# GpSimd's two passes over each converted weight piece are made as two half-width operations each

## The chip, the cores and the metric

The kernel runs on one core of a Trainium2 chip. The metric is the device time of one execution in microseconds; the median of three runs of the kernel before is 585.58 us.

## The reference

Three stages follow each other on 3072 tokens of 256 features. All is computed in float32 precision; the weights of the last two stages arrive as float64 numbers.

```python
# 1. decayed linear attention, chunk by chunk (batch 4, 8 heads, 768 positions, head 32, state 16)
M = (C @ B.T) * exp(cum_i - cum_j) * causal
y = M @ x + (C @ state) * exp(cum)
state = exp(sum(log a)) * state + sum_j decay_j * outer(B_j, x_j)
# 2. a layer of three products and a maximum (256 -> 768 -> 256)
h = maximum(maximum(y @ w1, y @ w2), y @ w3);  z = h @ w_out
# 3. a layer with a rational function (256 -> 2048 -> 256)
h = z @ w_in
g = (a0 + a1*h + a2*h**2 + a3*h**3) / (1 + |b0|*|h| + |b1|*h**2 + 1e-6)
out = g @ w_out2
```

## The kernel before

The sequence is cut into six groups `g` of 128 positions in four batches, so a group is 512 tokens. Stage 1 (attention) runs first, for all groups, in units `u` of four heads: TensorE makes scores (`s`) and decay differences (`d`), ScalarE the exponential `e`, VectorE the product `m` (L503), TensorE the output `y` from `m`. The matmuls of stages 2 and 3 then run group by group: stage 2 in blocks of 128 features (`pg`, or `ph` for group 0, the maximum into `xa` on VectorE at L726, its high and low part `hhi`, `hlo`), stage 3 in 16 blocks `k` of 128 features (`ph`, the rational function, its parts `ghi`, `glo`, the output `po`). A product of two float32 numbers is made of three matmuls of high and low parts (L644 to L646).

The weights come in 28 pieces of 256 by 256 float64 numbers: nine of `w1` to `w3`, three of the first output matrix (`wo1`), eight of `win`, eight of the second output matrix (`wo2`). Each is loaded as 32-bit halves (`wraw`, three buffers) and turned into a float32 number `a` (tile `wa`, two buffers) and its parts `hi` and `lo`, in `plan_conv`. On 128 partitions and 512 columns a piece takes: ScalarE, absolute value of the upper half (L246); VectorE, clamp (L247); ScalarE, scaled lower half into `we` (L249); VectorE, shift and mask (L250) and sign (L253); GpSimd, integer add (L256); ScalarE, the high part (L257, recorded at the helper's L196); GpSimd, the low part (L258). In the text below these are the steps of a piece: the VectorE steps L247, L250 and L253, the add L256 and the low part L258. A piece's add needs its L253, its high part needs the whole add, its low part needs the high part. The `wa` buffer of a piece is free for the piece after next only when its low part is done.

The order on every engine is fixed when the program is built. `Plan.op` records each operation with an engine and a cost, reads and writes of tiles; `Plan.emit` then walks through time with these costs and picks on each engine, among the operations that are ready, the one that is due first. Two operations that write the same tile are kept in order. The attention's operations all stand ahead of those of stages 2 and 3; the pieces (phase None) may stand anywhere, and so they lie between the attention's operations and between those of the first group in stages 2 and 3. Each engine runs its list in order, so an operation whose input is late holds everything behind it.

Of the kernel before, what the change touches and what calls it, by code (L numbers as in the profile page):

```python
# [9 lines left out]
F32 = mybir.dt.float32  # L10
# [4 lines left out]
ALU = mybir.AluOpType  # L15
# [141 lines left out]
def decay_attention_max_moe_rational_moe(  # L157
# [19 lines left out]
    act, dve, pool, pe = nc.scalar, nc.vector, nc.gpsimd, nc.tensor  # L177
# [16 lines left out]
    def copy(e, o, i):  # L194
        if e is act:
            act.activation(out=o, in_=i, func=AF.Copy)  # L196
        else:
            e.tensor_copy(out=o, in_=i)
# [14 lines left out]
    def plan_conv(plan, tok, nm, src, k0, c0):  # L213

        if nm == "wo2":
            hi, lo = (lambda i=i: wsb[nm, k0 // 2][i] for i in range(2))
        else:
            hi, lo = (lambda i=i: wsb[nm][i][:, k0:k0 + 2, c0:c0 + 256] for i in range(2))
        shape = [128, 2, 256]
        wide = src.dtype != F32  # L220
        raw = plan.tile("wraw", 3, lambda: cvr.tile(shape + [2], U32, tag="wraw", name="wraw") if wide
                        else cvr.tile(shape, F32, tag="wraw", name="wst"))
        rows = slice(128 * k0, 128 * k0 + 256)
        if not wide:
            plan.op("dma", 0.73, lambda: nc.sync.dma_start(
                out=raw.t, in_=src[rows, c0:c0 + 256].rearrange("(k p) n -> p k n", p=128)), [], [raw])
            plan.op("act", 0.52, lambda: copy(act, hi(), raw.t), [raw], [tok])
            plan.op("pool", 1.23, lambda: pool.tensor_tensor(out=lo(), in0=raw.t, in1=hi().bitcast(F32),
                                                             op=ALU.subtract), [raw], [tok])
            return  # L230
        a = plan.tile("wa", 2, lambda: cva.tile(shape, U32, tag="wa", name="wa"))
        e = plan.tile("we", 2, lambda: cve.tile(shape, U32, tag="we", name="we"))
        af = lambda: a.t.bitcast(F32)
        low, high = (lambda: raw.t[:, :, :, 0]), (lambda: raw.t[:, :, :, 1])
        raws[0] += 1
        first = f"w{raws[0]}" in FIRST

        plan.op("dma", 1.46, lambda: nc.sync.dma_start(
            out=raw.t.rearrange("p k n t -> p k (n t)"),
            in_=src.bitcast(U32)[rows, 2 * c0:2 * c0 + 512].rearrange("(k p) n -> p k n", p=128)), [], [raw],
            FIRST.index(f"w{raws[0]}") - 1000.0 if first else 6.0 + PIECE * raws[0],
            behind=[cum_t] if raws[0] < 4 and not first else ())
        plan.op("act", 0.67, lambda: act.activation(out=af(), in_=high().bitcast(F32), func=AF.Abs), [raw], [a])  # L246
        plan.op("dve", 0.41, lambda: dve.tensor_scalar(  # L247
            out=af(), in0=af(), scalar1=F64_LOW, scalar2=F64_HIGH, op0=ALU.max, op1=ALU.min), [], [a])
        plan.op("act", 0.67, lambda: act.activation(out=e.t, in_=low(), func=AF.Copy, scale=2.0 ** -29), [raw], [e])  # L249
        plan.op("dve", 0.41, lambda: dve.tensor_scalar(  # L250
            out=a.t, in0=a.t, scalar1=3, scalar2=0x3FFFFFF8,
            op0=ALU.logical_shift_left, op1=ALU.bitwise_and), [], [a])
        plan.op("dve", 0.68, lambda: dve.scalar_tensor_tensor(  # L253
            out=a.t, in0=high(), scalar=0xC0000000, in1=a.t,
            op0=ALU.bitwise_and, op1=ALU.bitwise_or), [raw], [a])
        plan.op("pool", 1.3, lambda: pool.tensor_tensor(out=a.t, in0=a.t, in1=e.t, op=ALU.add), [e], [a])  # L256
        plan.op("act", 0.6, lambda: copy(act, hi(), af()), [a], [tok])  # L257
        plan.op("pool", 1.3, lambda: pool.tensor_tensor(out=lo(), in0=af(), in1=hi().bitcast(F32),  # L258
                                                        op=ALU.subtract), [a], [tok])

    for nm in ("w1", "w2", "w3"):
        w_alloc(nm, KD, DF1)
# [3 lines left out]
    plan = Plan()  # L266
    op = plan.op
# [36 lines left out]
    def w_piece(nm, src, k0, c0):  # L304
        wt[nm, k0, c0] = mark()
        plan_conv(plan, wt[nm, k0, c0], nm, src, k0, c0)
# [53 lines left out]
    for i in range(2):  # L360
        for f in range(2):
            e = "dve" if f else "pool"
# [41 lines left out]
    for p in range(3):  # L404
        src = pcv if p == 0 else (lambda p=p: cr(p - 1))
        op("act", 0.3, lambda p=p, src=src: copy(act, cs[:, p], src()), [pc if p == 0 else cr_t], [cs_t])
        if p < 2:
            op("dve", 0.34, lambda p=p, src=src: dve.tensor_tensor(out=cr(p), in0=src(), in1=cs[:, p],
                                                                   op=ALU.subtract),
# [8 lines left out]
    def load_cum(g):  # L418
# [12 lines left out]
        out=sel.rearrange("r (q n f) -> r q n f", q=2, f=4),  # L431
# [160 lines left out]
    for s in range(NS_ALL + LEAD + 3):  # L592
# [5 lines left out]
        if 0 <= u < NS_ALL:  # L598
            g, k = divmod(u, NU)
# [8 lines left out]
        if 0 <= u < NS_ALL:  # L608
            g, k = divmod(u, NU)
# [63 lines left out]
    for s in range(NG * F2 + OL):  # L673
        g, k = divmod(s, F2)
# [287 lines left out]
```

## Time and profile before

| what | value |
|---|---|
| median of three runs (lowest, highest) | 585.58 us (583.31, 587.23) |
| profiled execution: time, span | 585.64 us, 583.9 us |
| busy share: PE, PEld, DVE, ACT, POOL | 96%, 71%, 90%, 75%, 73% |
| chain that ended last | PE 52%, DVE 21%, POOL 14%, issue 5%, DMA 4% |

PE is TensorE, PEld its weight loads, DVE is VectorE, ACT ScalarE, POOL GpSimd, SP the engine that issues the transfers. Busy shares are means over stages with different limits: the steps of the pieces lie between 10 and 157 us, and from there on the three other engines work beside a TensorE that has no gap up to 525 us. The span is 1.74 us shorter than the execution's time. Rows name the line of the kernel, the engine, the operation, and the output and input tiles.

### The profile page before, as it was taken

Reading aid. Unit: us, or ns where it says so; the run is one execution under the profiler, and the core shown is the slowest. Engines: PE = TensorE matmul, PEld = TensorE weight load, DVE = VectorE, ACT = ScalarE, POOL = GpSimd, SP = SyncE. Lnnn points to the kernel's source line nnn. Section 1 sums busy time; section 2 is a strip of 40 time slices with the busy share of each in tenths; the row PEclk is TensorE's granted clock in tenths of the full one; section 3 lists DMA queues with packets and bytes.
Section 4 is the critical chain, followed back from the end, with each engine's and each line's share of the span. In section 5 each row is a group of like instructions: output and inputs, shape, how many; then the busy total and the mean of one; then the engine's idle time right before and its main releaser. Section 6 shows DMA issues by size and latency. Waiting matters only on the chain.

```text
span 583.9 us, 8072 instructions
## 1 busy us (share of the span) xinstructions
PE 562.1 (96%) x2758; PEld 412.9 (71%) x2758; DVE 525.6 (90%) x775; ACT 436.8 (75%) x756; POOL 424.5 (73%) x354
## 2 busy tenths in 40 slices
PE   8988998899899999999999999999999999999997
PEld 3334343677688888888888888888888888886663
DVE  6999999699799989989889889989898889988996
ACT  5675777565678787878777877788787776788883
POOL 2565576488778867696667777687767997869983
PEclk9998999999999999999999999999999999999999
DMA  7885774533000000100000001000000010000000
GB/s 235 241 276 189 242 241 140 179 112 108 0 1 0 27 12 0 37 0 20 19 1 36 1 0 38 1 1 36 1 0 2 1 37 0 1 0 33 5 0 36
DMA packets 19043, 33.70 MB, mean 58 GB/s; under 512 B 3523, under 2 KB 4027, under 8 KB 19003
## 3 DMA queue, kind: packets, MB, share of 16 engines
q1 hardware_dynamic: 19003, 33.20, 17.7%
q8 instruction: 21, 0.34, 0.3%
q14 instruction: 19, 0.16, 0.1%
HBM read 27.27 MB, written 5.91 MB: 57 GB/s over the span
## 4 chain that ended last, share of the span: by engine, by line
PE 52%; DVE 21%; POOL 14%; issue 5%; DMA 4%; ACT 2%; SPq 1%; POOLq 0%; DVEq 0%; ACTq 0%
PE pg L644 7%; PE pg L645 7%; PE pg L646 7%; PE ph L644 5%; PE ph L645 5%; PE ph L646 5%; PE po L645 5%; PE po L646 5%; PE po L644 4%; DVE wa L253 2%; POOL glo L847 2%; DVE wa L247 2%; DVE wa L250 2%; DVE m L503 2%; POOL v L813 2%
## 5 line engine op out<-in xcount | busy, mean ns | idle before, releaser
L847 POOL TENSOR_TENSOR glo<-w,ghi 128x512 fp32r<-128x512 f32 x80 | 105.5, 1319 | 26.7 <-ACT ghi L196 26.7
L644 PE MATMUL pg<-xhi,w_hi 128*128 128x512 f32 x202 | 79.1, 392 | 2.2 <-DVE xa L726 1.6
L645 PE MATMUL pg<-xlo,w_hi 128*128 128x512 f32 x202 | 78.7, 390 | 0.0
L646 PE MATMUL pg<-xhi,w_lo 128*128 128x512 f32 x202 | 78.6, 389 | 0.0
L196 ACT ACTIVATE ghi<-w 128x512 fp32r<-128x512 f32 x80 | 50.5, 632 | 26.5 <-PE po L646 18.3
L834 ACT ACTIVATE pr<-v,qc 128x512 f32<-128x512 f32 x83 | 57.3, 691 | 17.5 <-POOL v L813 11.1
L256 POOL TENSOR_TENSOR wa<-wa,we 128x512 uint32<-128x512 uint32 x28 | 36.9, 1316 | 43.2 <-DVE wa L253 43.2
L291 POOL TENSOR_TENSOR hlo<-xa,hhi 128x512 fp32r<-128x512 f32 x36 | 50.3, 1398 | 20.2 <-ACT hhi L196 20.1
L644 PE MATMUL ph<-yhi,win_hi 128*128 128x512 f32 x160 | 62.5, 391 | 1.5 <-DVE w L832 1.5
L645 PE MATMUL ph<-ylo,win_hi 128*128 128x512 f32 x160 | 62.4, 390 | 0.8 <-DVE ylo L291 0.8
L645 PE MATMUL po<-glo,wo_hi 128*128 128x512 f32 x160 | 62.4, 390 | 0.4 <-POOL glo L847 0.4
L644 PE MATMUL po<-ghi,wo_hi 128*128 128x512 f32 x160 | 62.3, 389 | 0.0
L646 PE MATMUL ph<-yhi,win_lo 128*128 128x512 f32 x160 | 62.2, 389 | 0.0
L646 PE MATMUL po<-ghi,wo_lo 128*128 128x512 f32 x160 | 62.2, 389 | 0.0
L839 DVE SCALAR_TENSOR_TENSOR pr<-w,co,pr 128x512 f32<-128x512 f32 x83 | 62.0, 747 | 0.0
L813 POOL TENSOR_TENSOR v<-t,v 128x512 f32<-128x512 f32 x44 | 57.9, 1317 | 2.8
L836 DVE SCALAR_TENSOR_TENSOR v<-v,pr 128x512 f32<-128x512 f32 x83 | 56.3, 679 | 3.4 <-ACT pr L835 3.4
L841 DVE SCALAR_TENSOR_TENSOR w<-v,pr 128x512 f32<-128x512 f32 x83 | 56.4, 679 | 0.7
L835 ACT ACTIVATE pr<-pr 128x512 f32<-128x512 f32 x86 | 50.5, 588 | 1.0
L726 DVE TENSOR_TENSOR xa<-xa,pg 128x512 f32<-128x512 f32 x67 | 45.5, 679 | 3.8 <-ACT xa L196 2.7
L644 PEld LDWEIGHTS pg<-xhi,w_hi 128*128 128x128 f32 x202 | 37.9, 188 | 11.8 <-DVE xa L726 2.4
L646 PEld LDWEIGHTS pg<-xhi,w_lo 128*128 128x128 f32 x202 | 37.9, 188 | 7.9
(166 smaller groups left out, 1484.4 us busy)
## 6 DMA issues: line engine op xcount, KB each, us to landing
wraw<-in_wo_dram SPq DMA_DIRECT2D x11, 512.0 KB
wraw<-in_w_dram SPq DMA_DIRECT2D x9, 512.0 KB
wraw<-in_win_dram SPq DMA_DIRECT2D x8, 512.0 KB
xn<-in_xn_dram SPq DMA_DIRECT2D x6, 512.0 KB
out_dram<-ob SPq DMA_DIRECT2D x12, 256.0 KB
xt_d<-xo SPq DMA_DIRECT2D x10, 256.0 KB
xst<-xt_d SPq DMA_DIRECT2D x10, 256.0 KB
bt<-in_bz_dram SPq DMA_DIRECT2D x6, 256.0 KB
```

Source lines behind the costliest of these rows:

```text
L196: act.activation(out=o, in_=i, func=AF.Copy)
L291: lambda: e.tensor_tensor(out=lo.t, in0=src(), in1=hi.t.bitcast(F32), op=ALU.subtract),
L644: pe.matmul(dst, wh, hi, start=first, stop=False)
L645: pe.matmul(dst, wh, lo, start=False, stop=False)
L646: pe.matmul(dst, wl, hi, start=False, stop=last)
L813: pop(1.23, lambda: pool.tensor_tensor(out=f(v), in0=f(t1), in1=f(v), op=ALU.mult), [t1], [v])
L834: aop(0.62, lambda: act.activation(out=f(r), in_=f(v), func=AF.Ln, bias=qc), [v], [r])
L835: aop(0.48, lambda: act.activation(out=f(r), in_=f(r), func=AF.Exp, scale=-1.0), [], [r])
L836: dop(0.61, lambda: dve.scalar_tensor_tensor(out=f(v), in0=f(v), scalar=QC, in1=f(r), op0=ALU.add, op1=ALU.mult), [r], [v])
L839: dop(0.61, lambda: dve.scalar_tensor_tensor(out=f(r), in0=f(w), scalar=c(0), in1=f(r), op0=ALU.add, op1=ALU.mult), [w], [r])
L841: dop(0.61, lambda: dve.scalar_tensor_tensor(out=f(w), in0=f(v), scalar=2.0, in1=f(r), op0=ALU.subtract, op1=ALU.mult), [v, r], [w])
L847: pop(1.23, lambda: pool.tensor_tensor(out=f(lo), in0=f(w), in1=f(hi).bitcast(F32), op=ALU.subtract), [w, hi], [lo])
```

## The change

The add and the low part of a piece, one GpSimd operation of 512 columns each, are made as two of 256 columns each. The loop index `k` picks the half along the tile's middle axis. The recorded cost is 0.7 for each half where it was 1.3 for the whole. The halves of one step write the same tile, so the plan keeps them in order, but it may put other operations between them. The high part still waits for both halves of the add.

```diff
-        plan.op("pool", 1.3, lambda: pool.tensor_tensor(out=a.t, in0=a.t, in1=e.t, op=ALU.add), [e], [a])
+
+        for k in range(2):
+            plan.op("pool", 0.7, lambda k=k: pool.tensor_tensor(
+                out=a.t[:, k], in0=a.t[:, k], in1=e.t[:, k], op=ALU.add), [e], [a])
         plan.op("act", 0.6, lambda: copy(act, hi(), af()), [a], [tok])
-        plan.op("pool", 1.3, lambda: pool.tensor_tensor(out=lo(), in0=af(), in1=hi().bitcast(F32),
-                                                        op=ALU.subtract), [a], [tok])
+        for k in range(2):
+            plan.op("pool", 0.7, lambda k=k: pool.tensor_tensor(
+                out=lo()[:, k], in0=af()[:, k], in1=hi()[:, k].bitcast(F32), op=ALU.subtract), [a], [tok])
```

Lines behind the change stand four lower in the changed kernel (L503 becomes L507, L726 becomes L730); its add is L258 and its low part L262.

The plan's walk is taken with other costs and more operations, so the orders change on all engines up to the first blocks of stage 3. On GpSimd, early in the attention, the order before takes the pieces one after the other, add (L256) and low part (L258); `ct` is an operation of the attention:

```order
L256 TENSOR_TENSOR wa_205<-wa_205,we_210 128x512
L258 TENSOR_TENSOR w1_lo_87<-wa_205,w1_hi_86 128x2x256
L256 TENSOR_TENSOR wa_255<-wa_255,we_270 128x512
L258 TENSOR_TENSOR w2_lo_89<-wa_255,w2_hi_88 128x2x256
L256 TENSOR_TENSOR wa_310<-wa_310,we_283 128x512
L453 TENSOR_TENSOR ct_324<-ct_324,e0_368 128x512
```

At the same place the changed order is this (add L258, low part L262):

```order
L258 TENSOR_TENSOR wa_205<-wa_205,we_210 128x256 x2
L262 TENSOR_TENSOR w1_lo_87<-wa_205,w1_hi_86 128x256 x2
L258 TENSOR_TENSOR wa_255<-wa_255,we_271 128x256 x2
L262 TENSOR_TENSOR w2_lo_89<-wa_255,w2_hi_88 128x256
L258 TENSOR_TENSOR wa_312<-wa_312,we_284 128x256
L262 TENSOR_TENSOR w2_lo_89<-wa_255,w2_hi_88 128x256
```

The second half of the second piece's low part now stands behind the first half of the third piece's add. In the same way, a second half of a low part stands behind a half of the next piece's add at nine of the 28 pieces, six of them in the attention.

On VectorE, at the end of the attention (last `m`) and the begin of stage 2 (`xa`), the order before is:

```order
L253 SCALAR_TENSOR_TENSOR wa_1299<-wraw_1184,wa_1299 128x512
L247 TENSOR_SCALAR wa_1310<-wa_1310 128x512
L503 TENSOR_TENSOR m_1333<-s_1301,e_1322 128x512
L250 TENSOR_SCALAR wa_1310<-wa_1310 128x512
L503 TENSOR_TENSOR m_1340<-s_1302,e_1325 128x512
L253 SCALAR_TENSOR_TENSOR wa_1310<-wraw_1215,wa_1310 128x512
L726 TENSOR_TENSOR xa_1431<-xa_1431,pg_1419 128x512
```

There the changed order has, up to its first `xa`:

```order
L507 TENSOR_TENSOR m_1338<-s_1318,e_1322 128x512
L250 TENSOR_SCALAR wa_1315<-wa_1315 128x512
L507 TENSOR_TENSOR m_1354<-s_1319,e_1336 128x512
L253 SCALAR_TENSOR_TENSOR wa_1315<-wraw_1189,wa_1315 128x512
L247 TENSOR_SCALAR wa_1371<-wa_1371 128x512
L250 TENSOR_SCALAR wa_1371<-wa_1371 128x512
L253 SCALAR_TENSOR_TENSOR wa_1371<-wraw_1244,wa_1371 128x512
L730 TENSOR_TENSOR xa_1456<-xa_1456,pg_1440 128x512
```

The three steps of the last piece ahead of stage 2 now stand together, with no `m` between them, and that piece is the 19th and not the 20th.

## Rows read from the trace of the kernel before

**Rows 1.** Busy time by stretch: us, PE (x), PEld, DVE, ACT, POOL, clock, DMA, GB/s

```profile
14.00:109.00 95.00, 84.85 (x731) 36.38 (x731) 91.41 (x136) 67.28 (x120) 56.62 (x43) 0.98 0.66 207
109.00:160.00 51.00, 46.47 (x198) 36.29 (x197) 43.05 (x50) 31.89 (x55) 39.05 (x30) 1.00 0.34 113
189.00:525.00 336.00, 336.00 (x1484) 278.29 (x1483) 303.73 (x448) 262.31 (x447) 256.80 (x212) 1.00 0.03 12
```

**Rows 2.** What TensorE waited for, 14 to 109 us: total, times, longest

```profile
PE y L514 <- DVE m L503: 5.8, 8, 1.1
PE s L471 <- DVE m L503: 1.4, 2, 1.2
PE d L482 <- DVE st L567: 1.2, 2, 0.7
```

**Rows 3.** VectorE's costliest groups, 14 to 109 us: busy, mean ns, idle before

```profile
L503 DVE TENSOR_TENSOR m<-s,e 128x512 f32<-128x512 f32 x47 | 31.2, 679 | 0.4 <-PE s L471 0.4
L253 DVE SCALAR_TENSOR_TENSOR wa<-wraw,wa 128x512 uint32<-128x512 uint32 x19 | 18.1, 953 | 0.1
L250 DVE TENSOR_SCALAR wa<-wa 128x512 uint32<-128x512 uint32 x19 | 17.7, 930 | 0.1
L247 DVE TENSOR_SCALAR wa<-wa 128x512 f32<-128x512 f32 x19 | 15.7, 829 | 1.6 <-ACT wa L246 1.6
```

**Rows 4.** The tile `wa`, whole span: shortest, median and longest in ns

```profile
L247 DVE TENSOR_SCALAR wa<-wa x28: 411/952/1495, 11.0 to 147.6; 128x512 f32<-128x512 f32 x28
L250 DVE TENSOR_SCALAR wa<-wa x28: 410/900/1518, 11.9 to 148.7; 128x512 uint32<-128x512 uint32 x28
L253 DVE SCALAR_TENSOR_TENSOR wa<-wraw,wa x28: 673/692/1805, 12.9 to 149.2; 128x512 uint32<-128x512 uint32 x28
L256 POOL TENSOR_TENSOR wa<-wa,we x28: 1263/1278/1650, 13.7 to 151.1; 128x512 uint32<-128x512 uint32 x28
```

**Rows 5.** Timelines of GpSimd and VectorE around 42 us: start, us

```profile
41.59 1.27 POOL L258 TENSOR_TENSOR w_lo<-wa,w_hi 128x512 fp32r<-128x512 f32 x1 [0.74 <-ACT w_hi L196]
42.82 1.46 POOL L453 TENSOR_TENSOR ct<-ct,e 128x512 f32<-128x512 f32 x1
...
42.09 1.06 DVE L250 TENSOR_SCALAR wa<-wa 128x512 uint32<-128x512 uint32 x1
```

**Rows 6.** GpSimd's groups by form, whole span: the shape of a half

```profile
L804 POOL TENSOR_TENSOR hhi<-hlo,hhi 128x256 f32<-128x256 f32 x1 | 0.7, 733 | 0.0
```

**Rows 7.** GpSimd's groups, 14 to 109 us: the add

```profile
L256 POOL TENSOR_TENSOR wa<-wa,we 128x512 uint32<-128x512 uint32 x19 | 25.3, 1330 | 34.1 <-DVE wa L253 34.1
```

**Rows 8.** Timelines of GpSimd and VectorE in stage 2 of group 0

```profile
127.27 1.48 POOL L291 TENSOR_TENSOR hlo<-xa,hhi 128x512 fp32r<-128x512 f32 x1
128.71 1.48 POOL L258 TENSOR_TENSOR wo_lo<-wa,wo_hi 128x512 fp32r<-128x512 f32 x1
130.83 1.28 POOL L256 TENSOR_TENSOR wa<-wa,we 128x512 uint32<-128x512 uint32 x1 [0.63 <-DVE wa L253]
132.06 1.46 POOL L291 TENSOR_TENSOR hlo<-xa,hhi 128x512 fp32r<-128x512 f32 x1
...
128.11 0.92 DVE L250 TENSOR_SCALAR wa<-wa 128x512 uint32<-128x512 uint32 x1
129.07 1.68 DVE L253 SCALAR_TENSOR_TENSOR wa<-wraw,wa 128x512 uint32<-128x512 uint32 x1
```

**Rows 9.** VectorE's groups, 109 to 160 us

```profile
L253 DVE SCALAR_TENSOR_TENSOR wa<-wraw,wa 128x512 uint32<-128x512 uint32 x9 | 12.9, 1435 | 0.2
L247 DVE TENSOR_SCALAR wa<-wa 128x512 f32<-128x512 f32 x8 | 8.6, 1073 | 1.3 <-ACT wa L246 1.3
L250 DVE TENSOR_SCALAR wa<-wa 128x512 uint32<-128x512 uint32 x8 | 7.4, 930 | 0.1
```

**Rows 10.** What TensorE waited for, 109 to 160 us

```profile
PE ph L644 <- DVE w L832: 1.5, 1, 1.5
```

**Rows 11.** What ScalarE waited for, 14 to 160 us

```profile
ACT wa L246 <- POOL wo_lo L258: 3.9, 5, 2.6
```

## Prediction

> **What bounds the kernel now.** I read the busy times by stretch first. From 189 to 525 us TensorE has no gap [rows 1], so whatever happens there on the other engines is hidden, and the end moves only by what TensorE gains or loses before. The pieces end at 157 us. Two stretches are left: the attention (14 to 109 us) and stage 2 of group 0 with the first blocks of stage 3 (109 to 160 us). In the attention VectorE is busy for 91.41 of 95 us and TensorE for 84.85 [rows 1], and what TensorE waits for is VectorE: 5.8, 1.4 and 1.2 us, 8.4 in all [rows 2]. So VectorE sets the pace, and TensorE is next at 10 us less.
>
> Then I looked at what VectorE does there. Its largest group, `m`, takes 679 ns each, with no spread to speak of. The three steps of a piece take 829, 930 and 953 ns on the mean [rows 3], while the shortest of each are 411, 410 and 673 [rows 4]. The difference is not work. The timelines show what it is: the step L250 begins at 42.09, beside a GpSimd operation that runs from 41.59 to 42.86, and ends at 43.15, 0.29 us after it; the next GpSimd operation, which starts at 42.82, is the one that is lengthened, to 1.46 us [rows 5]. A VectorE step of a piece that meets a running GpSimd operation waits for its end, and the two then change places. No step waits longer than one operation lasts: the longest exceed the shortest by 1.08, 1.11 and 1.13 us [rows 4], the add lasts 1.26.
>
> The Trainium skill says the same ("SBUF — State Buffer", "Who interferes with whom"): VectorE in a two-port mode, or with two inputs in SBUF, shares a port pair with GpSimd, whoever starts first holds it for its whole instruction, and the other fully blocks. The trace agrees in these waits of at most 1.13 us.
>
> In the attention the waits sum to 19 x (0.418 + 0.520 + 0.280) = 23.1 us [rows 3, 4], or 0.406 a step over 57 steps. From 109 to 160 us they are 8 x 0.662 + 8 x 0.520 + 9 x 0.762 = 16.4 us [rows 4, 9].
>
> **What halves cost GpSimd.** The trace has 256-column operations of two inputs: 733 ns [rows 6]. Two are 1.466 us, against a median of 1.278 for the whole [rows 4]: 0.19 us more a step, 0.38 a piece, 10.5 over 28 pieces. In the attention GpSimd is busy for 56.62 of 95 us [rows 1] and idle for 34.1 ahead of the adds, waiting for L253 [rows 7]; 19 x 0.38 = 7.1 us hide in that as time on the engine. They do not hide as time of a piece, which is at least 0.38 longer from its L253 to the release of its buffer.
>
> **What they give VectorE in the attention.** A step that comes at a random moment meets GpSimd at work with a chance of 56.62/95 = 0.60 and waits half an operation, 0.65 us: 0.39. The rows say 0.406, so this simple view holds here. After the change the chance is (56.6 + 7.1)/95 = 0.67 and half an operation is 0.37 us: 0.245. That takes 0.16 from each of 57 steps: 9.2 us. The order takes one more piece away from this stretch: the 19th is the last ahead of the first `xa`, where it was the 20th. That is 829 + 930 + 953 ns, 2.7 us. VectorE comes down to 91.4 - 11.9 = 79.5 us, and TensorE with 84.85 is then the bound. If TensorE filled the stretch as well as VectorE does now (91.41/95 = 0.962), it would last 88.2 us, a gain of 6.8. That is the upper end in this view; the lower is nothing, since both engines run a fixed list and each step of a piece is also a link in a chain over four engines. This chain grows: by 0.38, and at six pieces in the attention by the wait of a low part's second half behind the next piece's add, which needs that piece's L253. ScalarE's absolute value for the piece after next is behind it, and in the same list the exponentials that `m` needs; ScalarE waits for the low part for 3.9 us now [rows 11]. I take two thirds of the gain, nearer to the upper end because the row that is largest, VectorE at 96%, is the one that is relieved: **-4.5 us**, ends 0 and -6.8.
>
> **Stage 2 of group 0.** Here the view is another. The rows show a cycle: a `hlo` at 127.27 and the next at 132.06, 4.79 us [rows 8]. In it GpSimd runs `hlo`, a low part and an add one behind the other, and its one gap, 0.63, is L253, which itself had waited for the low part (1.68 us from 129.07, to 0.56 after the low part's end). So the cycle is GpSimd's three operations and the VectorE steps that hold it up, end to end. Here a shorter operation lets a VectorE step in sooner, but the sum on the shared path stays, and it grows by 0.38: to 5.17 us. TensorE needs less than either: 336.0/1484 = 0.226 us a matmul at the most [rows 1], 18 of them in a cycle, 4.1 us. Against that the order has five pieces between the `xa`s where it had six: 5 x 5.17 = 25.9 us in place of 6 x 4.79 = 28.7. Two follow ahead of the first rational block, before and now, and the pieces left over go beside stage 3, where VectorE and GpSimd have 32 and 79 us free [rows 1]. Ends: -2.8 from this count, +2.3 (six times 0.38) if the number of pieces does not matter because the `hlo`s set the cycle alone. I take **-0.5**, near the middle, since no row prefers one end.
>
> **First blocks of stage 3.** TensorE waits 1.5 us for the first rational result [rows 10], which comes from GpSimd's L831. Ahead of it now stand three halves, 3 x 0.733 = 2.2 us, of the last pieces but one, where one low part of 1.75 stood: **+0.5**.
>
> Sum: 585.64 (the profiled execution, 0.06 from the median of the runs) - 4.5 - 0.5 + 0.5 = 581.1; I say **581**. The ends of the terms give 585.64 + 0 + 2.3 + 0.5 = 588.4 and 585.64 - 6.8 - 2.8 + 0 = 576.
>
> **Rivals.**
>
> Full relief: VectorE's waits go by more than half, because a piece's add begins right behind its L253 and the next step comes about 0.7 us later, behind one `m`: at the end of the first half, not in the middle of it. Then TensorE's 8.4 us [rows 2] go, and with them a good part of the 4 us of gaps in stage 2 (51 - 46.47 [rows 1]): 585.6 - 8.4 - 3 = 574. For it speaks that VectorE is so clearly the bound; against it that a fixed order always leaves gaps, and that the operations met are met where the plan puts them.
>
> No gain: the second half, queued behind the first, takes the port pair again before the waiting VectorE step. Then a step waits as long as now, the add is 0.19 longer, and the time is 585.6 to 588 (six cycles of 0.38 in stage 2). For it speaks the rule of the skill page just named, in its wording: who starts first holds the pair, with nothing on who is next. Against it speaks the one place above, where GpSimd's next operation was recorded as started at 42.82 and VectorE was done at 43.15 all the same [rows 5].
>
> Slower: the second half of a low part, behind the next piece's add, waits for VectorE's L253. The add's wait for L253 is 34.1/19 = 1.8 us on the mean [rows 7]; at six places in the attention that holds `wa`, then ScalarE's list, then `m` and TensorE: 6 x 1.8 = 10.8 us. VectorE's order now also has the three steps of some pieces in one block with no `m` between, which makes `m` late by up to two steps, 0.41 + 0.67 us. If more than about half of the 10.8 reaches TensorE, the 4.5 us are gone; if all does and the relief is small, the time is 592. Against it: the `m`s follow in blocks of three to five behind such pieces, so the order leaves time there.
>
> Not done: were the halves merged or run whole, the time would be 585.6. The order of the built program shows them apart, so this hardly counts.
>
> **How the numbers follow.** Chances: forecast (577 to 585) 0.44, full relief 0.24, no gain 0.14, slower 0.15, not done 0.03. One per cent, 5.9 us, is about what a measurement of this kernel can tell from no change: faster means below 579.7. That is the full relief and a third of the forecast's case, 0.39; slower is the slower case, 0.15; the rest, 0.46, is within one per cent. The range, 8 in 10, runs from 572 (a little past full relief) to 590, which leaves out about half of the slower case and the tail below.
>
> **What would show it.** In the changed trace: halves of about 0.73 us; means of the steps near 0.66, 0.70 and 0.85 us in the attention and no wait over 0.75 us; VectorE's busy share below TensorE's from 14 us to the first `xa`; that first `xa` some 4 us earlier; ScalarE's waits for low parts above 3.9 us. In stage 2 a cycle near 5.2 us. I am wrong if VectorE's waits are short and TensorE's gaps are not (the chain through GpSimd bounds the attention), if the waits stay (the port goes to the second half), or if the change shows behind 189 us.

## The result and the profile after

The changed kernel takes 580.61 us (median of six runs, 578.88 to 581.21) against 585.85 us of the kernel before, beside which it was timed. The ratio is 0.9906, 95% interval 0.9886 to 0.9927: 5.2 us less, 0.4 us from the forecast. The profiled execution has a span of 579.0 us, 4.9 less than before.

The first view is the busy time by stretch, here cut at two events that both traces have: the first maximum `xa` on VectorE, and the end of TensorE's wait for the first rational block. This is before (us from start to end, length, PE with count, PEld, DVE, ACT, POOL, clock, DMA share, GB/s):

```profile
14.00:112.10 98.10, 87.95 (x744) 38.93 (x744) 91.85 (x136) 68.52 (x122) 58.46 (x45) 0.98 0.67 210
112.10:159.50 47.40, 42.90 (x183) 33.31 (x181) 42.11 (x48) 30.19 (x52) 36.80 (x28) 1.00 0.30 103
159.50:583.90 424.40, 419.68 (x1796) 335.87 (x1796) 382.18 (x573) 330.17 (x569) 326.85 (x277) 1.00 0.03 12
```

And this is after, cut at the same two events:

```profile
14.00:105.80 91.80, 88.08 (x750) 38.10 (x749) 80.14 (x134) 68.11 (x120) 63.89 (x76) 0.98 0.70 226
105.80:152.40 46.60, 41.67 (x179) 32.87 (x177) 36.03 (x49) 29.42 (x52) 40.11 (x45) 1.00 0.30 102
152.40:579.00 426.60, 421.63 (x1796) 336.87 (x1796) 385.82 (x577) 331.75 (x572) 335.05 (x284) 1.00 0.04 12
```

The attention ends 6.3 us earlier, stage 2 of group 0 with the first block is 0.8 us shorter, and the rest, with the same 1796 matmuls, is 2.2 us longer. In the attention VectorE's busy time falls by 11.7 us although GpSimd's rises by 5.4. TensorE, busy for 88 of 98 us before, is busy for 88 of 92 now.

VectorE's groups from 14 to 109 us answer to [rows 3] (busy, mean ns, idle before, and what ended it):

```profile
L507 DVE TENSOR_TENSOR m<-s,e 128x512 f32<-128x512 f32 x47 | 31.1, 681 | 5.5 <-PE s L475 4.1 <-ACT xo L196 0.7 <-ACT e L502 0.5
L253 DVE SCALAR_TENSOR_TENSOR wa<-wraw,wa 128x512 uint32<-128x512 uint32 x19 | 16.0, 841 | 0.2
L247 DVE TENSOR_SCALAR wa<-wa 128x512 f32<-128x512 f32 x19 | 13.1, 692 | 5.8 <-ACT wa L246 5.7
L250 DVE TENSOR_SCALAR wa<-wa 128x512 uint32<-128x512 uint32 x19 | 10.4, 545 | 0.2
```

The three steps take 2.08 us together and not 2.71; the shortest are as before, so the waits fell from 1.22 to 0.58 us a piece. `m` is unchanged, but it is now VectorE that waits for TensorE (4.1 us) and for ScalarE's absolute value (5.7). What TensorE waited for in the same stretch answers to [rows 2] (total, times, longest):

```profile
PE y L518 <- DVE m L507: 1.0, 3, 0.4
PE d L486 <- DVE st L571: 0.9, 2, 0.7
PE d L453 <- ACT e L502: 0.7, 1, 0.7
PE d L486 <- ACT e L456: 0.6, 1, 0.6
PE d L486 <- ACT e L502: 0.5, 1, 0.5
```

Of the 8.4 us that TensorE waited for VectorE there, 1.9 are left, but it now waits for ScalarE's exponentials for 1.8 us. All its idle time from 14 us to the first `xa` falls from 10.2 us (98.10 - 87.95) to 3.7 (91.80 - 88.08), about as much as the stretch gains.

Six steps of a piece in the changed kernel still waited for about 1 us (1.0 to 1.1 above their shortest), two of them in the attention. Each of the six began beside a GpSimd operation that the change leaves whole (`ct`, `hlo` or `v`), as here, where L247 lasts 1.51 us and its shortest is 0.41:

```profile
113.39 1.31 POOL L295 TENSOR_TENSOR hlo<-xa,hhi 128x512 fp32r<-128x512 f32 x1
113.47 1.51 DVE L247 TENSOR_SCALAR wa<-wa 128x512 f32<-128x512 f32 x1 [1.32 <-ACT wa L246]
```

The 2.2 us that are given back show in TensorE's timeline (start, us, count) and in short stretches of the same columns as above:

```profile
150.01 0.39 PE L650 MATMUL pg<-xhi,w_lo 128*128 128x512 f32 x1
152.46 0.56 PE L648 MATMUL ph<-yhi,win_hi 128*128 128x512 f32 x1 [2.05 <-DVE w L836]
152.81 0.63 PE L649 MATMUL ph<-ylo,win_hi 128*128 128x512 f32 x1
153.24 0.63 PE L650 MATMUL ph<-yhi,win_lo 128*128 128x512 f32 x1
...
155.80 0.57 PE L650 MATMUL pg<-xhi,w_lo 128*128 128x512 f32 x1
156.21 0.39 PE L648 MATMUL pg<-xhi,w_hi 128*128 128x512 f32 x1
```

```profile
154.00:156.00 2.00, 2.00 (x6) 1.52 (x5) 2.00 (x4) 0.63 (x2) 2.00 (x3) 0.50 0.00 0
156.00:158.00 2.00, 2.00 (x10) 1.62 (x9) 2.00 (x5) 0.84 (x2) 0.96 (x2) 0.96 0.00 0
```

After a wait of 2.05 us (1.5 before [rows 10]) the granted clock stands at 0.50, the 1.2 GHz level, until about 156 us. The matmuls then start 0.43 us apart and not 0.23; nine of them, from 152.46 to 156.21, cost 1.7 us more. In the trace of before no such drop followed the 1.5 us. Both traces also have one drop in the attention. Of the six runs of the changed kernel two, the profiled one among them, have a mean clock of 0.994 and the others 0.996 or 0.997; 0.003 of 579 us is 1.7 us, so the second drop may belong to some executions and not to the change as such. Only one of them was profiled, so this is not shown.

### The profile page after: what moved, and what is told of

Same layout as the page of the kernel before. It is cut to its first block, busy times and chain, and to the rows that moved or that the text cites. A ratio compares the mean times of both kernels' runs of the same rounds, so it can differ in the third digit from the quotient of the medians.

```text
span 579.0 us, 8171 instructions
## 1 busy us (share of the span) xinstructions
PE 562.4 (97%) x2758; PEld 412.4 (71%) x2758; DVE 510.5 (88%) x775; ACT 436.6 (75%) x756; POOL 441.1 (76%) x410
## 4 chain that ended last, share of the span: by engine, by line
PE 55%; POOL 17%; DVE 16%; issue 4%; ACT 3%; DMA 3%; SPq 1%; POOLq 0%; DVEq 0%; ACTq 0%
PE pg L648 6%; PE pg L649 6%; PE pg L650 6%; PE ph L648 4%; PE ph L650 4%; PE ph L649 4%; PE po L649 4%; PE po L650 4%; PE po L648 4%; PE s L475 3%; POOL glo L851 2%; PE d L488 2%; POOL hlo L295 2%; POOL v L817 2%; PE d L486 2%
## 5 line engine op out<-in xcount | busy, mean ns | idle before, releaser
L258 POOL TENSOR_TENSOR wa<-wa,we 128x256 uint32<-128x256 uint32 x56 | 44.2, 800 | 31.1 <-DVE wa L253 31.1
L730 DVE TENSOR_TENSOR xa<-xa,pg 128x512 f32<-128x512 f32 x67 | 45.5, 680 | 3.3 <-PE pg L650 3.0
L835 POOL TENSOR_TENSOR w<-w,t 128x512 f32<-128x512 f32 x20 | 25.9, 1295 | 24.0 <-DVE v L824 22.1
```

## The experiments

Two causes were mixed in the change, shorter holds of the shared path (my theory) and another order on all engines (the rival: one piece less in the attention, two beside stage 3). The runs part them. All ratios are to the kernel before in the same session, whose medians were 585.4 to 586.3 us.

| run | ratio (95% interval) | median, us | `xa`, us |
|---|---|---|---|
| the change | 0.9906 (0.9886 to 0.9927) | 580.61 | 105.8 |
| e1: its order, whole operations | 0.9931 (0.9907 to 0.9954) | 581.92 | 110.6 |
| e2: old order, halves | 0.9945 (0.9924 to 0.9967) | 582.25 | 108.9 |
| e3: old order, quarters | 1.0181 (1.0162 to 1.0201) | 596.24 | 116.8 |
| e4: cost 1.6, whole | 0.9949 (0.9930 to 0.9969) | 581.99 | 108.8 |
| e5: cost 1.6, halves | 0.9907 (0.9876 to 0.9938) | 579.57 | 108.8 |
| e6: old order, low part in halves | 0.9972 (0.9949 to 0.9995) | 584.48 | 107.2 |
| e7: old order, add in halves | 0.9988 (0.9967 to 1.0008) | 584.81 | 111.1 |
| e8: pieces due later, whole | 0.9948 (0.9931 to 0.9966) | 582.65 | 104.9 |
| e9: pieces due later, halves | 0.9963 (0.9944 to 0.9981) | 584.07 | 105.9 |
| e10: cost 1.8, halves | 0.9985 (0.9968 to 1.0002) | 584.77 | 105.1 |
| e11: cost 1.4, whole (control) | 0.9972 (0.9951 to 0.9993) | 584.12 | 111.4 |
| e12: cost 1.2, whole (control) | 1.0032 (1.0007 to 1.0057) | 588.15 | 109.6 |

The last column is the start of the first maximum with a `pg` input in the one profiled execution, 112.1 before. That execution is the shortest of its version in e3, e6, e8 and e12 and the longest in e1 and e5, so the column does not rank the versions.

**e1, the changed order with whole operations.**

```diff
         for k in range(2):
-            plan.op("pool", 0.7, lambda k=k: pool.tensor_tensor(
-                out=a.t[:, k], in0=a.t[:, k], in1=e.t[:, k], op=ALU.add), [e], [a])
+            plan.op("pool", 0.7, lambda k=k: pool.tensor_tensor(out=a.t, in0=a.t, in1=e.t, op=ALU.add)
+                    if k else None, [e], [a])
```

(and the low part in the same way)

> The changed kernel's order on every engine, but the add and the low part run as whole 512-column operations: at the place of a first half nothing is issued, at the place of the second half the whole. If the shorter hold of GpSimd is the cause (my theory), VectorE's steps wait as long as before the change (sum of the three means near 2.7 us in the attention, against 2.08 with halves) or longer, and the time is within 3 us of the kernel before: 583 to 589 us. If the new order is the cause (rival: one piece less in the attention, two pieces beside stage 3), the gain stays: 579 to 582 us.

Measured 0.9931: the order alone keeps most of the gain. My theory fails as the only cause. What the halves add to this order is not shown by this pair, since the intervals of e1 and of the change overlap. VectorE's groups of e1, 14 to 109 us:

```profile
L253 DVE SCALAR_TENSOR_TENSOR wa<-wraw,wa 128x512 uint32<-128x512 uint32 x19 | 17.2, 906 | 0.2
L247 DVE TENSOR_SCALAR wa<-wa 128x512 f32<-128x512 f32 x18 | 16.6, 919 | 2.5 <-ACT wa L246 2.4
L250 DVE TENSOR_SCALAR wa<-wa 128x512 uint32<-128x512 uint32 x18 | 12.2, 679 | 0.2
```

The steps sum to 2.50 us, between before (2.71) and after (2.08): the order itself takes away a sixth of the 1.22 us of waits, a third of what the change takes. L250 is 0.25 us shorter on the mean, with a median in the whole run of 427 ns, close to its shortest (407); L247 is 0.09 us longer.

In time the order does more for TensorE than its late `xa` (110.6) suggests. Its idle time from 14 us to the first `xa` is 5.2 us in e1 (91.41 busy of 96.60), against 10.2 before and 3.7 in the change. But in this execution, the longest of e1's six, the granted clock stood at the 1.2 GHz level from about 88 to 98 us, with TensorE busy all the time (stretches of two us, columns as above):

```profile
92.00:94.00 2.00, 2.00 (x12) 0.40 (x10) 1.29 (x2) 0.62 (x2) 1.91 (x2) 0.50 0.86 267
94.00:96.00 2.00, 2.00 (x14) 0.84 (x6) 0.00 (x0) 1.49 (x4) 0.58 (x1) 0.50 0.44 165
```

That is some 5 us of clock lost (0.51 from 88 to 98.5), where the drops in the attention before (0.83 from 50 to 60) and after (0.59 from 88 to 92) lost some 1.7 each. The six runs of e1 go with their mean granted clock, from 578.45 us at 0.999 to 582.95 at 0.990.

**e2, halves in the old order.**

```diff
-        plan.op("pool", 1.3, lambda: pool.tensor_tensor(out=a.t, in0=a.t, in1=e.t, op=ALU.add), [e], [a])
+        plan.op("pool", 1.3, lambda: [pool.tensor_tensor(
+            out=a.t[:, k], in0=a.t[:, k], in1=e.t[:, k], op=ALU.add) for k in range(2)], [e], [a])
```

(and the low part in the same way)

> The order and the costs of the kernel before; each add and each low part is issued as two halves that follow each other at once. My theory: VectorE's steps wait less, as in the changed kernel, sum of the three means in the attention 2.0 to 2.2 us against 2.71 before, first maximum 3 to 6 us earlier, 580 to 583 us. Rival (the order is the cause): 584 to 588 us. Rival (the second half takes the port again): means as before.

Measured 0.9945, with an `xa` 3.2 us earlier: the halves alone gain too, as expected. The rows of `wa` (whole span: shortest, median, longest ns) decide whether the second half takes the path again here:

```profile
L256 POOL TENSOR_TENSOR wa<-wa,we x56: 720/734/1177, 14.6 to 148.3; 128x256 uint32<-128x256 uint32 x56
L247 DVE TENSOR_SCALAR wa<-wa x28: 414/852/1020, 11.9 to 144.2; 128x512 f32<-128x512 f32 x28
L250 DVE TENSOR_SCALAR wa<-wa x28: 408/760/958, 12.9 to 144.8; 128x512 uint32<-128x512 uint32 x28
L253 DVE SCALAR_TENSOR_TENSOR wa<-wraw,wa x28: 672/680/1240, 13.8 to 145.7; 128x512 uint32<-128x512 uint32 x28
```

The longest waits are now 0.61, 0.55 and 0.57 us (1.08 to 1.13 before [rows 4]), less than one half's 0.73, though two halves stand back to back: a waiting step gets in between. The same shows in the cycle of stage 2 that [rows 8] had, here in e2's timelines:

```profile
119.02 1.48 POOL L293 TENSOR_TENSOR hlo<-xa,hhi 128x512 fp32r<-128x512 f32 x1
120.45 2.06 POOL L259 TENSOR_TENSOR wo_lo<-wa,wo_hi 128x256 fp32r<-128x256 f32 x2
122.48 1.43 POOL L256 TENSOR_TENSOR wa<-wa,we 128x256 uint32<-128x256 uint32 x2
123.88 1.48 POOL L293 TENSOR_TENSOR hlo<-xa,hhi 128x512 fp32r<-128x512 f32 x1
...
120.82 1.10 DVE L253 SCALAR_TENSOR_TENSOR wa<-wraw,wa 128x512 uint32<-128x512 uint32 x1
```

L253 now lasts 1.10 and not 1.68 us. It runs between the two halves of the low part, whose pair lasts 2.06 us with it, and the add follows without the gap of 0.63. The cycle is 4.86 us here.

**e3, quarters in the old order** (as e2, with `for k in range(2) for c in (0, 128)` and 128 columns each).

> As with the halves in the old order, but four operations of 128 columns each. My theory: VectorE's waits fall further, but by the two 256-column and 512-column rows each further operation costs GpSimd 0.19 us, so a quarter is about 0.46 us and a whole step 1.84 instead of 1.28; a piece is 1.1 us longer on GpSimd, and where GpSimd and VectorE hold each other up in turn (stage 2 of group 0) the cycle grows from 4.8 to 5.9 us. 583 to 590 us, slower than halves in the old order by 2 to 7. If only VectorE's waits count, it is faster than halves: 577 to 580.

Measured 1.0181, slower than before by some 10.6 us, more than expected (the cycle of stage 2 is 5.4 us, less than expected). VectorE's steps hardly wait any more (0.56, 0.48 and 0.81 us on the mean to 109 us), and still `xa` comes 4.7 us later than before. VectorE's largest wait in e3 from 14 to 160 us, which was 2.8 us in 3 times before:

```profile
DVE wa L247 <- ACT wa L246: 22.3, 21, 1.9
```

The absolute value comes late because its buffer does: a quarter lasts 456 ns on the median, four of them 1.8 us, and a piece is 1.1 us longer on GpSimd before it frees its `wa`. ScalarE's absolute values wait for low parts for 20.8 us from 14 to 160 us (4.4 before). VectorE no longer waits for the path but for the next piece. By these waits the two buffers of `wa` are the bound here; no run had a third one to show it.

**e4, one number in the plan: cost 1.6, operations whole.**

```diff
-        plan.op("pool", 1.3, lambda: pool.tensor_tensor(out=a.t, in0=a.t, in1=e.t, op=ALU.add), [e], [a])
+        plan.op("pool", 1.6, lambda: pool.tensor_tensor(out=a.t, in0=a.t, in1=e.t, op=ALU.add), [e], [a])
```

(and the low part in the same way)

> The kernel before with one number changed: the plan's cost of the add and of the low part is 1.6 and not 1.3. The operations stay whole and in one place. The order that follows has 19 pieces (not 20) ahead of the first maximum and 26 (not 28) ahead of stage 3, as the changed kernel's, but no halves between other work. If the order's part of the gain comes from pieces that are put off to where TensorE hides them, 581 to 583 us. If it comes from where the changed order sets single operations, the time is that of before, 584.5 to 587.

Measured 0.9949, 581.99 us, in the middle of the first expectation. Nothing in the work changed; 19 and 26 pieces instead of 20 and 28 stand ahead of the two points.

**e5, cost 1.6 and halves issued together** (e2's two operations with 1.6).

> Cost 1.6 as in the last kernel, and each add and low part issued as two halves that follow each other at once. If the shorter holds and the put-off pieces are two causes, this has both: 578 to 581 us, as the changed kernel or better, since no low part's half stands behind the next piece's add. If the interleaved halves are needed, 582 to 584.

Measured 0.9907, the change's own ratio, without its interleaved halves. What the change adds to e4 and e2 is therefore not the place of single halves. That halves gain on top of put-off pieces is likely from e5 beside e4, but the intervals just overlap.

**e6 and e7, one of the two steps in halves, old order** (e2's edit for the low part alone, and for the add alone).

> Order and costs of before; only the low part runs as two halves at once, the add is whole. In stage 2's cycle it is the low part that L253 waits for, and the add that L247 waits for; so here L253's mean falls (from 0.95 to about 0.8 us in the attention) and L247's stays near 0.83. The add, on the way to the high part, is not lengthened. About half of what both halves gave in this order (3.1 us): 583 to 585 us.

> Order and costs of before; only the add runs as two halves at once, the low part is whole. L247's mean falls (0.83 to about 0.7 us), L253's stays near 0.95. About half of the 3.1 us again, or less, because the add's 0.19 us more is on the way to the high part: 583 to 586 us.

Measured 0.9972 and 0.9988; the second interval holds 1. The means moved as expected, in ns to 109 us: with the low part in halves L253 836 and L247 797, with the add in halves L253 926 and L247 705. L250, of which nothing was expected, moved as much, from 930 to 719 and to 811. Together they make e2's 0.9945 within the intervals. The low part seems worth more, but the intervals overlap.

**e8 and e9, pieces due later** (`PIECE = 4.0` for 2.6, cost 1.3; e8 whole, e9 halves).

> The kernel before with one other number changed: the due time from piece to piece is 4.0 us and not 2.6, costs stay 1.3 and the operations whole. The order has 17 pieces (not 20) ahead of the first maximum and 25 (not 28) ahead of stage 3. If putting pieces off is what the order gives, the gain is that of cost 1.6 or more: 579 to 583 us, first maximum at 106 to 108 us. If cost 1.6 helped for another reason (the plan's GpSimd times come nearer to the chip's), 585 to 588.

> Due time 4.0 us a piece, as in the last, and both steps in halves issued together. With both causes at work and three pieces put off: 576 to 580 us. If the late pieces now hold up stage 3 (its outputs need the last pieces), 581 to 586, with TensorE waiting behind 160 us.

e8 gave 0.9948, as cost 1.6 did, with whole operations at the old cost: put-off pieces gain by a second way of making them. In e9 the halves gave nothing on top (0.9963, the intervals overlap); the time is that of its second expectation. TensorE does wait behind 160 us there, as that expectation has it, for 1.95 us at 195 and 0.90 at 204 (0.70 and 0.60 in e8), beside the 2.50 at 154. What TensorE waited for in e8 from 10 to 200 us shows the next bound:

```profile
PE ph L644 <- DVE w L832: 3.5, 2, 2.8
PE pg L644 <- DVE xa L726: 3.2, 2, 1.7
```

The first `xa` is 7.3 us earlier than before, earlier than the 106 to 108 us expected, but the first rational block's wait has grown from 1.5 to 2.8 us; of the 7.3 us 4.5 are left in the span. In e9 TensorE waited for VectorE's `w` for 4.5 us (2.50 and 1.95).

**e10, cost 1.8 and halves** (e5 with 1.8).

> Both steps in halves issued together, planned at a cost of 1.8 each: 16 pieces ahead of the first maximum, 25 ahead of stage 3. The trend from cost 1.3 (582.3) and 1.6 (579.6) goes on: 576 to 580 us, or turns because pieces then crowd stage 2 of group 0, where GpSimd has no room: 580 to 584 us, with a longer time between the first maximum and stage 3.

Measured 0.9985, 584.77 us: it turned, as the second expectation has it, and somewhat further than its 584. One wait of TensorE's in e10 is longer than the whole gain of the change:

```profile
PE ph L647 <- POOL hlo L293: 7.4, 1, 7.4
```

Nine pieces, 17 to 25, stand between the two points (eight before, seven in the change), and on GpSimd the last `hlo` stands behind two adds and two low parts in a row. In the stretch from 138 to 150 us the granted clock is 0.57.

**e11 and e12, controls: other orders with no piece put off** (cost 1.4 and 1.2, whole).

> A control for the order: plan's cost 1.4 instead of 1.3, operations whole. The order changes in many places, but as before 20 pieces stand ahead of the first maximum and 28 ahead of stage 3. If the order's gain comes from pieces put off, there is none here: 584.5 to 587.5 us. If the order before was merely an unlucky one, so that most others are faster, 581 to 583.5.

> A second control: cost 1.2, operations whole, 20 and 28 pieces at the same two points, again another order in between. Put-off pieces as the cause: 584.5 to 587.5 us, as the kernel before. An unlucky order before: 581 to 583.5.

Measured 0.9972 and 1.0032, 584.12 and 588.15 us: one between its two expectations, one above both; a little faster and a little slower than before, both outside 1 by a hair. So a reshuffle alone is worth some 0.3% either way. The three orders with put-off pieces and whole operations (e1, e4, e8) are at -0.5 to -0.7%, beyond both controls, but their intervals overlap that of e11.

The profile of e12 is of its shortest run, 583.12 us of a median of 588.15. In it TensorE's idle time from 14 us to `xa` is 6.4 us, 3.7 less than before, with no piece put off. Its other runs differ in the mean granted clock: the two at 0.997 and 0.994 took 583.12 and 583.81 us, the ten at 0.980 to 0.991 took 587.13 to 591.29. So a part of the difference between versions seems to lie in how often the clock drops in them, and the controls do not settle what an order is worth by itself. No run held the clock fixed.

## Why the prediction was right

**The bound.** VectorE at 96% set the attention's pace and TensorE was next, 10 us below the length of the stretch (its busy time was 6.6 us below VectorE's; "10 us less" mixes the two). Right: VectorE lost 11.7 us of busy time (forecast 11.9), TensorE's waits for VectorE fell from 8.4 to 1.9, and VectorE now waits for TensorE. The stretch shrank by 6.3 us; I took 4.5 with an upper end of 6.8. The step of two thirds was too careful: I held a part back for the longer chain of a piece. That chain did grow, the largest of ScalarE's waits for low parts from 14 to 160 us being these [rows 11]:

```profile
ACT wa L246 <- POOL wo_lo L262: 6.0, 4, 4.0
ACT wa L246 <- POOL win_lo L262: 3.8, 4, 1.9
```

and VectorE waited for absolute values for 10.8 us instead of 2.8. It seems to have cost little because TensorE was by then the busier engine; no run tests this.

**The waits.** Half an operation, half the wait: forecast 0.245 us a step, measured 0.58/3 = 0.19. But e1 shows that a part of this is the order's. In the same old order (e2) the steps sum to 2.11 us, 0.20 us of wait each; so the halves account for nearly all of it when alone, and order and halves overlap when together. In the sum I gave 9.2 of 11.9 us to the halves and 2.7 to the piece put off. The trace of the change does not bear this out: from 14 us to the first `xa` the steps' waits fell from 23.1 to 11 us (19 steps of 841, 18 of 706 and 18 of 552 ns), by 12 and not 9.2; one L247 and one L250 less give 0.8, and other operations of VectorE grew by 1.2. That 11.7 is so near to 11.9 is in part luck. In time the runs give the halves 0.55%, the order 0.69%, both 0.94%; that this is less than their sum of 1.24% is not clear of the intervals. The total was right, the split was not: the order was undervalued. The sign "no wait over 0.75 us" failed too, behind the operations that stay whole. The waits from 109 to 160 us sum to 16.3 and not 16.4 us, which changes nothing.

**GpSimd's price.** Halves of 0.737 us on the median (forecast 0.733). It hid, as said, in GpSimd's idle time. e3 shows where it stops hiding.

**Stage 2.** The cycle was to grow to 5.17 us. It is 19.33/4 = 4.83 from the first `hlo` to the fifth, with seven halves of adds between them and not eight:

```profile
108.73 1.48 POOL L295 TENSOR_TENSOR hlo<-xa,hhi 128x512 fp32r<-128x512 f32 x1 [0.60 <-ACT hhi L196]
...
117.08 1.43 POOL L258 TENSOR_TENSOR wa<-wa,we 128x256 uint32<-128x256 uint32 x2 [0.63 <-DVE wa L253]
...
127.36 0.74 POOL L258 TENSOR_TENSOR wa<-wa,we 128x256 uint32<-128x256 uint32 x1 [0.69 <-DVE wa L253]
128.06 1.30 POOL L295 TENSOR_TENSOR hlo<-xa,hhi 128x512 fp32r<-128x512 f32 x1
```

4.79 before by the same count, 4.81 in e2. The term of 0.38 was mis-sized. In e2 the halves let L253 run inside the low part, and the gap of 0.63 us that it used to cause closes, which pays for the longer operations. In the change it closes in two of the four cycles and stays in the other two (0.63 and 0.69 above). The stretch gained 0.8 us, the wait at its end included; forecast -0.5 and +0.5. That wait grew by 0.55 (forecast +0.5). The three halves stand there as forecast, but with VectorE's steps between them they last 3.2 us and not 2.2, and with the same order and whole operations (e1) the wait is 0.89 us, so the size agrees in part by luck.

**After 152 us.** I forecast nothing there, and 2.2 us came back, 1.7 of them as a lower clock in this execution. The forecast sum was near because this met the undersized gain of the attention. That is luck: by stretch the profile has -6.3, -0.8 and +2.2 us where I had -4.5, 0 and 0. Against other executions the attention's gain and the end cannot be matched, since only one is profiled.

**Rivals.** Full relief: its condition held, VectorE's waits went by more than half (1.22 to 0.58 us a piece), and it came true in the attention (1.9 of 8.4 us of waits left), but not in the total. The second half did not take the path again (e2). The slower case did not show in the change; a piece that frees its buffer late, as it has it, is by the waits what made the quarters slow.

What stays open: whether the order's gain is only the put-off pieces. e1, e4 and e8 speak for it, but e11, which puts off none, has half of that gain, and the granted clock differs between the versions. And why halves gain nothing on top of pieces due later (e9) is seen in one execution only: TensorE's two later waits are 1.55 us longer than in e8, one of them after a single step L250 of 2.99 us (see the end). No version beat the change; e5 equals it.

## What to carry to other kernels

Where two engines share a path by turns, as VectorE and GpSimd here, the wait of the one is set by the length of the other's operations (one step in e9 apart): read each operation's shortest and mean time, and where they differ on the busy engine, shorten the other's operations, though the total work grows. Watch where the longer chain begins to hold its buffers: halves gained, quarters lost three times as much. And when a planner sets the order, run the new order with the old operations and the old order with the new operations before giving the gain to either, and compare the granted clocks of the runs.

## What was not expected of the hardware

With halves queued back to back (e2) no VectorE step of a piece waited for longer than one half: 0.61 us at the most, where a half lasts 0.73. So no gap between the halves is needed for a waiting step to get in. One step on record did not get in. In e9 an L250 starts at 186.16 us and lasts 2.99, while GpSimd runs two whole operations one behind the other, `glo` from 186.32 to 187.62 and `hlo` from 187.57 to 188.87; it ends 0.28 us after the second. In every other version the longest wait is at most 1.15 us. What was different there is not known.

In the changed kernel a wait of TensorE of 2.05 us was followed by some 3.5 us at the 1.2 GHz level, which cost 1.7 us more in matmuls. At the same place of the program waits of 2.81 us (e8) and 2.50 us (e9) were followed by none: the granted clock stayed at 1.00 there. In these three executions the length of the wait alone does not decide.

The runs of the kernel before hardly go with their mean granted clock (584.86 us at 0.984 and at 0.997), those of several faster versions do (e5: 577.79 us at 1.000, 582.08 at 0.991). That fits a TensorE whose lost clock was hidden behind VectorE and no longer is, but no run separates the two.
